# Linear attention, then a mixture of four experts, on one core: values of one chunk and scores of the next in one step, and other dummy products

## The chip, the cores and the metric

The kernel runs on one core of a Trainium2 chip, as one launch. The metric is the device time in microseconds; a comparison takes the median of several runs. The time before is 1175.42 us, the median of three runs.

## The reference

The attention has 4 batches, 8 heads, 768 positions and 64 values a head, and runs over blocks of 64 positions with a state of 64x64 for each head. Its result, brought to 3072 tokens by 512, is the input x of four experts, whose outputs are weighted by normalised probabilities and added. All is float32.

```
for b in range(nb):
    intra = np.einsum('bhic,bhjc->bhij', qb, kb) * Dmask[None]
    intra = np.einsum('bhij,bhjd->bhid', intra, vb)
    inter = np.einsum('bhid,bhde->bhie', qb * lam_pow[None], kv_state)
    out[:, :, sl] = intra + inter
    kv_state = lam_block * kv_state + np.einsum('bhsd,bhse->bhde', kb * rev_pow, vb)
...
for e in range(E):
    h = np.maximum(x @ w1[e], 0.0)
    out += p[:, e:e + 1] * (h @ w2[e])
```

## The kernel before, in words

**Tiling.** The 3072 tokens are three groups of 1024, and a group is eight chunks of 128 positions (two blocks of the reference, all heads): chunks 0 to 7, 8 to 15 and 16 to 23. A unit is one group with one expert; there are twelve. The two products of the experts use recursive schemes with seven products in place of eight: `first_product` (line 974) computes x times w1 in 7 x 7 products, `second_product` (line 1028) the next one in 7, for the first two groups; the last group's second product is nested too (line 1256).

**Time in slots.** The loop over units has seven macro steps (index i) of eight slots (index x), so a unit has 56 slots. Even slots hold a part of the second product of this unit, odd slots a part of the first product of the next unit. Each part is eight records of 128x256 on TensorE, but slot 7, with four. After the parts of a slot, the loop takes at most a few items of vector work from lists (`lately` holds the attention's, `background` and `own_sums` others), then runs the list `steps`, where `attention(g)` has put each chunk's work by slot number.

**A chunk of groups 1 and 2** has these steps. `load_more` loads q and k, `load` loads v. `turn` transposes q and k by TensorE (line 603) into banks s0 and s1, from where ScalarE copies them to qT and kT (lines 611, 612); for chunks 16 to 23, which come through a DRAM tensor in pieces of 32, VectorE does it (`turn_across`, line 585). `decayed` scales k on GpSimd. `scores` does 64x64 products, four at a time in the quarters of the array: q times k (line 633) and the addition to the state (line 640), both into two banks, whose results VectorE masks into the tile st and adds to the state (`mask`, `middle`, `end`). `values` multiplies q scaled with the state (line 687) and st with v (line 705) into two banks; ScalarE copies the results to xc (line 726) and VectorE adds the rest, by the list `adds`, which is emptied at the start of the next step or in a later slot. After each second chunk `pair_sums` does four subtractions on GpSimd and sends the blocks to the DRAM tensor x_blocks (lines 744 to 746).

Before, chunk i of a group is turned at slot BEGIN[g][0] + BEGIN[g][1] * i. Its scores are 4 slots later (6 in group 2), its values 10 (12) slots later, all in banks s0 and s1. q and k are loaded 10 slots ahead of the turn, v 6 slots ahead. `scale_q` multiplies q by its decay: from the bank into a tile qs in group 1, after the transposes into qs in group 2, in both ahead of the scores.

**Operands of a group.** `x_fill` (line 352) loads a group's x from x_blocks on SP's queue, and GpSimd does four subtractions (`x_inner`). It runs in slot 3 of seven macro steps from FILL[g] on. The first product of group 1 begins in macro step 21, which is slot 169.

**Banks.** PSUM has eight banks here: g1 and g3 for the first product, q01, q02, q11, q12 for the second, s0 and s1 for the attention. In the second product, stages M7, M4 and M2 (macro steps 1, 2 and 4) use q02 and q12; the others use q01 and q11.

**Loads.** SP issues nearly all DMAs, in order. In slot 0 of each macro step `feed` loads an operand of w1 (ws_in, line 887) for a later step, ahead of what `steps` has for that slot. `small` takes tiles from a pool of 41 that all parts share.

**The start.** `warm` issues products of zeros on TensorE while the first loads are under way (line 448), ten at first, then three and two between the turns of chunks 0 and 1 and the first scores. Chunks 0 to 7 run ahead of and between the first large products, from a list written out by hand (lines 1436 to 1445).

Of the kernel before, what the change touches and what calls it, by code (L numbers as in the profile page):

```python
# [21 lines left out]
def kernel(  # L22
# [30 lines left out]
    nc = tc.nc  # L53
# [4 lines left out]
    P = nc.NUM_PARTITIONS  # L58
# [4 lines left out]
    CPG = 8  # L63
# [28 lines left out]
    def small(name):  # L92
        return pool.tile([P, W], FP32, name=name, tag="t")
# [44 lines left out]
    nat = {}  # L138
# [272 lines left out]
    def comes_across(n):  # L411
        return where(n)[0] >= SECOND
# [11 lines left out]
    def load_more(n):  # L424
        if not comes_across(n):
            load(n, "qk")
        else:
            trickle(sum(b <= where(n)[1] for b, _ in pieces))
            load_across(n)
            load(n, "k")  # L430
# [8 lines left out]
    load(3)  # L439


    zeros = small("zeros")[:, 0:P]
    nc.vector.memset(zeros, 0.0)

    def warm(n):
        p = bank("g1", "zp")
        for _ in range(n):
            nc.tensor.matmul(out=p[:, 0:P], lhsT=zeros, rhs=zeros, start=True, stop=True)

    warm(10)  # L450

# [32 lines left out]
    def scale_q(qs, of):  # L486
        by = q_decay.unsqueeze(2).to_broadcast([P, NHP, 2, BL])
        tt(nc.vector, by_block(qs), by_block(of), by, ALU.mult)
# [33 lines left out]
    turned, masked = {}, {}  # L522
# [4 lines left out]
    background = []  # L527
# [9 lines left out]
    def take(queue, force=False):  # L537
        for x, f in enumerate(queue):
            if force or getattr(f, "at", 0) <= now[0] and getattr(f, "can", lambda: True)():
                queue.pop(x)()  # L540
                return
# [8 lines left out]
    def soon(n, *work):  # L550

        if n < CPG:
            background[0:0] = work
            rest(len(work))
        else:
            lately.extend(work)

    def decayed(n):

        kn = nat[n, "k"]  # L560
        kd = kn if n >= CPG else small("kd")[:].rearrange("p (h d) -> p h d", d=D)
        nat[n, "kd"] = kd
        by = k_decay.rearrange("p r ac -> p ac r").unsqueeze(3).to_broadcast([P, NHP, 2, D])
        tt(nc.gpsimd, *(x.rearrange("p (ac r) d -> p ac r d", r=2) for x in (kd, kn)), by, ALU.mult)
# [10 lines left out]
    def turn_across(n):  # L575

        qT, kT = nat.pop((n, "qx")), nat.pop((n, "kx"))
        qs = small("qs")

        def scaled():  # L580
            scale_q(qs, qT)
            turned[n] = qT, kT, qs

        def across(x):
            nc.vector.transpose(out=x[:], in_=x[:])
            vector(W, False)

        soon(n, *(lambda x=x: across(x) for x in (qT, kT)), scaled)

    def turn(n, tags):  # L590
        all_added()
        begin_state(n)
        if comes_across(n):
            turn_across(n)
            return
        if n < CPG:
            decayed(n)
        qn, kn = nat.pop((n, "q")), nat[n, "k"]
        qp = bank(tags[0], "qp")
        kp = bank(tags[1], "kp")  # L600
        for x, y in ((qp, qn), (kp, kn)):
            for ac in range(NHP):
                nc.tensor.transpose(  # L603
                    out=x[:, ac * C:(ac + 1) * C], in_=y[:, 2 * ac:2 * ac + 2].rearrange("p r d -> p (r d)"),
                    identity=ident[:],
                )
        if n >= CPG:
            decayed(n)
        del nat[n, "k"]
        qT, kT, qs = small("qT"), small("kT"), small("qs")  # L610
        nc.scalar.copy(out=qT[:], in_=qp[:])
        nc.scalar.copy(out=kT[:], in_=kp[:])
        scaled = lambda: scale_q(qs, qp)
        soon(n, scaled)
        turned[n] = qT, kT, qs, scaled

    def scores(n, tags):
        all_added()
        while n not in turned:
            take(lately, True)  # L620
        qT, kT = turned[n][0:2]
        while any(f in lately for f in turned[n][3:]):
            take(lately, True)
        begin_state(n)
        kd, vn = nat.pop((n, "kd")), nat[n, "v"]
        first, last = where(n)[0] == 0, where(n)[0] == NCH - 1

        sp = [bank(tags[r], "sp") for r in range(2)]
        blk = [slice(x * BL, (x + 1) * BL) for x in range(2)]
        for ac in range(NHP):  # L630
            for r in range(2):
                for x in range(2):
                    nc.tensor.matmul(  # L633
                        out=sp[r][half[x], ac * BL:(ac + 1) * BL], lhsT=hc(kT)[half[r], ac, blk[x]],
                        rhs=hc(qT)[half[r], ac, blk[x]], start=(ac == 0), stop=True, skip_group_check=True,
                    )
        for ac in range(NHP):
            for x in range(1 if last else 2):
                for r in range(2):
                    nc.tensor.matmul(  # L640
                        out=sp[x][half[r], 256 + ac * D:256 + (ac + 1) * D], lhsT=kd[half[x], 2 * ac + r],
                        rhs=vn[half[x], 4 * r + ac], start=False, stop=True, skip_group_check=True,
                    )
        st = small("st")
        added = [sp[x][:, 256:512].rearrange("p (h d) -> p h d", d=D) for x in range(2)]

        def mask(r):
            tt(
                nc.vector, st[:, r * 256:(r + 1) * 256], sp[r][:, 0:256], s_decay[:, r].rearrange("p h c -> p (h c)"),
                ALU.mult,  # L650
            )

        def middle():
            s = states[n][:, 1]
            if first:
                nc.scalar.copy(out=s, in_=added[0])
            else:
                tt(nc.vector, s, s, added[0], ALU.add)

        def end():  # L660
            s = states[after_of(n)] = small("kv")[:].rearrange("p (x h d) -> p x h d", x=2, d=D)
            passed(nc.vector, s[:, 0], states[n][:, 1])
            tt(nc.vector, s[:, 0], s[:, 0], added[1], ALU.add)

        work = [lambda: (mask(0), mask(1)), middle] + ([] if last else [end])
        soon(n, *work)
        masked[n] = st, work

    def values(n, tags):
        all_added()  # L670
        vn = nat.pop((n, "v"))
        qs, *scaled = turned.pop(n)[2:]
        st, work = masked.pop(n)
        while any(f in lately for f in (*scaled, *work)):
            take(lately, True)
        while any(f in background for f in (*scaled, *work)):
            rest(force=True)
        state = states.pop(n)
        first = where(n)[0] == 0
# [67 lines left out]
            made.add(("blocks", g, x)),  # L747
        ))

    FILL = {1: 18, 2: 43}  # L750
    BEGIN = {1: (24, 13), 2: (8 * 19, 22)}
    steps = []

    def attention(g):

        def put(slot, f):
            steps.append((slot, f))

        for i in range(CPG):
            n, s = g * CPG + i, BEGIN[g][0] + BEGIN[g][1] * i  # L760
            put(s - 10, lambda n=n: load_more(n))
            put(s - 6, lambda n=n: load(n, "v"))
            put(s, lambda n=n: turn(n, ("s0", "s1")))
            if comes_across(n):
                put(s - 2, lambda n=n: (decayed(n), nat.pop((n, "k"))))
            put(s + (6 if comes_across(n) else 4), lambda n=n: scores(n, ("s0", "s1")))
            put(s + (12 if comes_across(n) else 10), lambda n=n: values(n, ("s0", "s1")))
            if n == 2 * CPG + 3:
                put(s + 17, turn_gates)
        steps.sort(key=lambda s: s[0])  # L770

    def forget():
# [656 lines left out]
    def loads(*of):  # L1429
        return lambda: [raw_w1(0, x) if isinstance(x, str) else load(x) for x in of]  # L1430
# [3 lines left out]

    h1, h2 = parts["M1"], parts["M2"]
    for f in (
        (ts[0], lambda: warm(3)), (ts[1], lambda: warm(2)), (ss[0], loads(4, 5)), (ss[1], loads("A21", 6)),
        (vs[0], loads("A22")), (vs[1], loads(7)), (ts[2],), (m1[0],), (ss[2],), (m1[2],),
        (vs[2],), (ts[3],), (h2[0][0],), (ss[3],), (ts[4],), (h2[0][1],),
        (vs[3],), (h2[2][0],), (ss[4],), (ts[5],), (h2[2][1], sum_first("S3", "A11", "A21")),  # L1440
        (vs[4],), (h1[1][0],), (ss[5],), (ts[6], sum_first("S1", "A21", "A22", ALU.add)), (h1[1][1],),
        (vs[5],), (h1[3][0],), (ss[6],), (ts[7], load_probs), (h1[3][1], sum_first("S2", "S1", "A11")),
        (vs[6],), (h2[1][0], sum_x(0)), (ss[7],), (h2[1][1], sum_first("S4", "A12", "S2")),
        (begin_chores, m2[3]), (vs[7],), (sum_x(1), quarter_5(0)), (quarter_5(2),),
    ):
        for work in f:
            work()
        now[0] += 1
        pump()
# [178 lines left out]
```

## Time and profile before

| what | us |
|---|---|
| median of three runs (lowest, highest) | 1175.42 (1170.89, 1178.54) |
| the profiled execution, its own time | 1171.55 |
| its span in the profile | 1169.8 |
| TensorE (PE) busy | 1157.8 |
| VectorE (DVE) busy | 791.7 |
| GpSimd (POOL) busy | 646.1 |
| ScalarE (ACT) busy | 271.1 |
| products of zeros, line 448, 30 records | 5.4 |
| transposes of q and k, line 603, 128 records | 19.7 |
| scores, lines 633 and 640, 1472 records | 32.7 |
| values, lines 687 and 705, 1472 records | 32.2 |

The span is that of one execution on the core; its own time is 1.75 us longer. A product in float32 shows as two records, a transpose as one. [...]eight of 128x256 have a mean of 0.38 us each, but start 0.21 us apart. The rate is therefore read from the chain of waits, which gives the time from one step to the next, and not from the mean of a record.

A line of the page's fifth part reads: line, engine, operation, written and read tiles, shapes, count, busy time, mean ns, idle time ahead of it and what ended it. A line of waits reads: engine, line, what it waited for, us in total, times, longest.

### The profile page before, as it was taken

To read this page: it belongs to the slowest core of one execution; us is meant where nothing else is said; L and a number is where in the kernel's file an instruction comes from. 1 tells how busy PE (TensorE), PEld (TensorE's weight loads), DVE (VectorE), ACT (ScalarE), POOL (GpSimd) and SP (SyncE) were. 2 spreads that over 40 slices of the span, in tenths; PEclk is the share of its full clock that TensorE was granted. 3 is DMA by queue.
4 is the path that set the end of the run, shared out by engine and by line. 5 is a ranking of instruction groups with operands and counts; after the bars stand their busy time and mean duration, and the time that the engine had idled before them with its cause. 6 is when DMAs were issued, how large, how long until landed. Compare 5 with 4: busy or idle time off the path is not lost.

```text
span 1169.8 us, 21185 instructions
## 1 busy us (share of the span) xinstructions
PE 1157.8 (99%) x8095; PEld 1006.5 (86%) x8095; DVE 791.7 (68%) x1407; ACT 271.1 (23%) x540; POOL 646.1 (55%) x640
## 2 busy tenths in 40 slices
PE   8999999999999999999999999999999999999998
PEld 7888888888888888888888888888888888888887
DVE  4666895578478567657747836745775666777785
ACT  4321122112211201211211120221233342341231
POOL 2846327546655761065245215655893683882884
PEclk9999999999999999999999999999999999999999
DMA  9884668998997996787868757785765445354442
GB/s 208 219 257 153 185 195 264 289 315 255 310 334 228 311 277 188 221 264 230 247 195 261 243 182 239 215 278 184 252 212 194 140 152 181 129 182 148 154 180 73
DMA packets 265717, 255.63 MB, mean 219 GB/s; under 512 B 121328, under 2 KB 219408, under 8 KB 265616
## 3 DMA queue, kind: packets, MB, share of 16 engines
q1 hardware_dynamic: 254976, 251.46, 69.0%
q10 hardware_dynamic: 10640, 2.82, 1.1%
q8 instruction: 64, 1.05, 0.4%
q14 instruction: 37, 0.30, 0.1%
HBM read 180.80 MB, written 77.61 MB: 221 GB/s over the span
## 4 chain that ended last, share of the span: by engine, by line
PE 95%; DVE 3%; POOL 1%; issue 0%; DMA 0%; ACTq 0%; ACT 0%; POOLq 0%; DVEq 0%
PE pg L974 39%; PE q L1028 31%; PE pq L1256 13%; PE pM L1358 2%; PE pc L1358 2%; DVE m L102 1%; PE sp L633 1%; PE op L687 1%; PE op L705 1%; PE sp L640 1%; PE qp L603 1%; PE kp L603 1%; POOL acc L102 1%; POOL m L102 1%; DVE sums L102 0%
## 5 line engine op out<-in xcount | busy, mean ns | idle before, releaser
L974 PE MATMUL pg<-xs,ws_in 128*128 128x256 f32 x1960 | 471.6, 380 | 0.8 <-DVE m L102 0.7
L1028 PE MATMUL q<-w2t,m 128*128 128x256 f32 x1792 | 424.4, 380 | 0.0
L974 PEld LDWEIGHTS pg<-xs,ws_in 128*128 128x128 f32 x1960 | 369.8, 190 | 53.7 <-DVE m L102 3.3
L102 DVE TENSOR_TENSOR m<-pg,m 128x512 f32<-128x512 f32 x451 | 307.2, 687 | 120.0 <-PE pg L974 109.8
L1028 PEld LDWEIGHTS q<-w2t,m 128*128 128x128 f32 x1792 | 339.3, 190 | 46.6 <-DVE m L102 0.4
L1046 DVE SCALAR_TENSOR_TENSOR acc<-q,gate,acc 128x256 f32<-128x256 f32 x192 | 92.3, 481 | 126.2 <-PE q L1028 125.7
L102 DVE TENSOR_TENSOR m<-m,m 128x512 f32<-128x512 f32 x184 | 152.5, 829 | 7.7 <-ACT m L986 7.7
L986 ACT ACTIVATE m<-m 128x512 f32<-128x512 f32 x132 | 83.0, 630 | 303.6 <-DVE m L102 302.5
L102 POOL TENSOR_TENSOR m<-m,decay 128x512 f32<-128x512 f32 x64 | 81.8, 1293 | 58.1 <-ACT m L986 44.7
L102 DVE TENSOR_TENSOR sums<-pq,sums 128x256 f32<-128x256 f32 x153 | 64.1, 421 | 45.7 <-PE pq L1256 36.9
L982 ACT COPY m<-pg 128x512 f32<-128x512 f32 x88 | 51.5, 585 | 186.1 <-PE pg L974 176.1
L1256 PE MATMUL pq<-acc,w2t 128*128 128x256 f32 x352 | 86.6, 379 | 0.0
L102 POOL TENSOR_TENSOR xs<-xs 128x256 f32<-128x256 f32 x56 | 44.5, 794 | 73.1 <-DMA xs<-x_blocks 57.4
L1256 PEld LDWEIGHTS pq<-acc,w2t 128*128 128x128 f32 x352 | 66.8, 190 | 9.3 <-issue 0.3
L102 POOL TENSOR_TENSOR to<-xc 128x256 f32<-128x256 f32 x16 | 12.5, 783 | 95.8 <-DVE xc L102 67.8
L102 POOL TENSOR_TENSOR acc<-hT,hT 128x512 f32<-128x512 f32 x32 | 40.2, 1269 | 29.7 <-PE pq L1256 27.8
L102 POOL TENSOR_TENSOR kn<-kn,decay 128x512 f32<-128x512 f32 x16 | 18.0, 1123 | 64.6 <-PE kp L603 43.7
L102 POOL TENSOR_TENSOR w2o<-w2b 128x512 f32<-128x512 f32 x32 | 42.4, 1348 | 18.3 <-DMA w2b<-in_moe_w_dram 10.2
L915 ACT ACTIVATE m<-m 128x512 f32<-128x512 f32 x44 | 27.7, 630 | 106.8 <-DVE m L102 106.8
L102 POOL TENSOR_TENSOR ops<-w2b 128x256 f32<-128x256 f32 x24 | 17.8, 764 | 50.7 <-issue 28.2
L102 POOL TENSOR_TENSOR acc<-hT,acc 128x512 f32<-128x512 f32 x32 | 40.7, 1271 | 7.4 <-PE pq L1256 5.4
L102 POOL TENSOR_TENSOR w2o<-w2b,w2o 128x512 f32<-128x512 f32 x24 | 34.2, 1449 | 5.8 <-issue 4.3
(135 smaller groups left out, 1204.8 us busy)
## 6 DMA issues: line engine op xcount, KB each, us to landing
ws_in<-w_ops SPq DMA_DIRECT2D x70, 896.0 KB, 6.3
w2t<-w_ops SPq DMA_DIRECT2D x66, 256.0 KB, 5.1
w2t<-w_sums SPq DMA_DIRECT2D x64, 256.0 KB, 3.7
w_ops<-ops SPq DMA_DIRECT2D x28, 512.0 KB, 4.3
w2t<-in_moe_w_dram SPq DMA_DIRECT2D x48, 256.0 KB, 3.6
w2b<-in_moe_w_dram SPq DMA_DIRECT2D x32, 256.0 KB, 5.5
w_sums<-w2o SPq DMA_DIRECT2D x16, 512.0 KB, 5.7
w2b<-in_moe_w_dram SPq DMA_DIRECT2D x16, 512.0 KB, 7.6
```

Source lines behind the costliest of these rows:

```text
L102: eng.tensor_tensor(out=o, in0=a, in1=b, op=op)
L603: nc.tensor.transpose(out=x[:, ac * C:(ac + 1) * C], in_=y[:, 2 * ac:2 * ac + 2].rearrange("p r d -> p (r d)"), identity=ident[:],)
L633: nc.tensor.matmul(out=sp[r][half[x], ac * BL:(ac + 1) * BL], lhsT=hc(kT)[half[r], ac, blk[x]], rhs=hc(qT)[half[r], ac, blk[x]], start=(ac ...
L640: nc.tensor.matmul(out=sp[x][half[r], 256 + ac * D:256 + (ac + 1) * D], lhsT=kd[half[x], 2 * ac + r], rhs=vn[half[x], 4 * r + ac], start=F ...
L915: nc.scalar.activation(out=o[:], in_=o[:], func=AF.Relu)
L974: nc.tensor.matmul(out=p[:, j * 256:(j + 1) * 256], lhsT=ws[i][:, j * P:(j + 1) * P], rhs=xs[i], start=(fresh and j == 0), stop=True, skip ...
L982: nc.scalar.copy(out=new[at][:], in_=p[:])
L986: nc.scalar.activation(out=new[at][:], in_=new[at][:], func=AF.Relu)
L1028: nc.tensor.matmul(out=p[:, s * DH:(s + 1) * DH], lhsT=h[A_OF[m]][:, c * 256 + s * P:c * 256 + (s + 1) * P], rhs=fed2[g, e, m][uu][:, c], ...
L1046: nc.vector.scalar_tensor_tensor(out=o, in0=x, scalar=w, in1=o, op0=ALU.mult, op1=ALU.add)
L1256: nc.tensor.matmul(out=p[:, 0:256], lhsT=fed3[e, m, x // 2][:, x % 2, c * P:(c + 1) * P], rhs=b[B_OF[i]][:, c * 256:(c + 1) * 256], start= ...
L1358: nc.tensor.matmul(out=p[:, s * 256:(s + 1) * 256], lhsT=a[c][:, f:f + P], rhs=b[:, c, j * 256:(j + 1) * 256], start=(s == 0 and c == 0 an ...
```

## The change

Three edits go together.

- The slots of scores of chunks 8 to 23 are written out in SCORES. For eleven chunks, `both` does the values of the chunk before and then the scores of this one, in one step; those scores use banks q02 and q12. Chunks 8 to 11 and 16 (ALONE) have their scores alone in s0 and s1, and values of a chunk ahead of those, or of a group's last, come 7 slots after its own scores. The turn comes 4 slots ahead of the scores (7 in group 2), q and k are loaded 7 slots ahead of the turn and v 2 slots ahead; in group 2 k is decayed 3 slots ahead of the turn. FILL[1] goes from 18 to 19.
- For chunks 8 to 23, q is scaled in place, from and to SBUF, as the last item of the scores' vector work. The mask writes over kT (over qT in chunks 0 to 7) instead of a tile of its own.
- The products of zeros are 512 columns wide instead of 128. There are three at first instead of ten, then one instead of three, and none instead of two.

```diff
-    zeros = small("zeros")[:, 0:P]
+    zeros = small("zeros")[:]
...
-            nc.tensor.matmul(out=p[:, 0:P], lhsT=zeros, rhs=zeros, start=True, stop=True)
-
-    warm(10)
+            nc.tensor.matmul(out=p[:], lhsT=zeros[:, 0:P], rhs=zeros, start=True, stop=True)
+
+    warm(3)
...
     def turn_across(n):
...
-        qs = small("qs")
-
-        def scaled():
-            scale_q(qs, qT)
-            turned[n] = qT, kT, qs
+        def ready():
+            turned[n] = qT, kT, qT
...
-        soon(n, *(lambda x=x: across(x) for x in (qT, kT)), scaled)
+        soon(n, *(lambda x=x: across(x) for x in (qT, kT)), ready)
...
     def turn(n, tags):
...
-        qT, kT, qs = small("qT"), small("kT"), small("qs")
+        qT, kT = small("qT"), small("kT")
+        qs = small("qs") if n < CPG else qT
...
-        scaled = lambda: scale_q(qs, qp)
-        soon(n, scaled)
-        turned[n] = qT, kT, qs, scaled
+        turned[n] = qT, kT, qs
+        if n < CPG:
+            soon(n, lambda: scale_q(qs, qp))
...
     def scores(n, tags):
...
-        st = small("st")
+        st = kT if n >= CPG else qT
...
         work = [lambda: (mask(0), mask(1)), middle] + ([] if last else [end])
+        if n >= CPG:
+            work.append(lambda: scale_q(qT, qT))
         soon(n, *work)
...
-    FILL = {1: 18, 2: 43}
-    BEGIN = {1: (24, 13), 2: (8 * 19, 22)}
+    FILL = {1: 19, 2: 43}
+    SCORES = {1: (28, 41, 54, 67, 82, 98, 114, 137), 2: (160, 194, 210, 226, 250, 266, 282, 306)}
+    ALONE = *range(CPG, CPG + 4), 2 * CPG
...
-        for i in range(CPG):
-            n, s = g * CPG + i, BEGIN[g][0] + BEGIN[g][1] * i
-            put(s - 10, lambda n=n: load_more(n))
-            put(s - 6, lambda n=n: load(n, "v"))
-            put(s, lambda n=n: turn(n, ("s0", "s1")))
+        def both(n, *tags):
+
+            values(n - 1, ("s0", "s1"))
+            scores(n, tags)
+
+        for i, s in enumerate(SCORES[g]):
+            n = g * CPG + i
+            early = 7 if comes_across(n) else 4
+            put(s - early - 7, lambda n=n: load_more(n))
+            put(s - early - 2, lambda n=n: load(n, "v"))
+            put(s - early, lambda n=n: turn(n, ("s0", "s1")))
             if comes_across(n):
-                put(s - 2, lambda n=n: (decayed(n), nat.pop((n, "k"))))
-            put(s + (6 if comes_across(n) else 4), lambda n=n: scores(n, ("s0", "s1")))
-            put(s + (12 if comes_across(n) else 10), lambda n=n: values(n, ("s0", "s1")))
+                put(s - early - 3, lambda n=n: (decayed(n), nat.pop((n, "k"))))
+            if n in ALONE:
+                put(s, lambda n=n: scores(n, ("s0", "s1")))
+            else:
+                put(s, lambda n=n: both(n, "q02", "q12"))
+            if n + 1 in ALONE or i == CPG - 1:
+                put(s + 7, lambda n=n: values(n, ("s0", "s1")))
             if n == 2 * CPG + 3:
-                put(s + 17, turn_gates)
+                put(s + 10, turn_gates)
...
-        (ts[0], lambda: warm(3)), (ts[1], lambda: warm(2)), (ss[0], loads(4, 5)), (ss[1], loads("A21", 6)),
+        (ts[0], lambda: warm(1)), (ts[1],), (ss[0], loads(4, 5)), (ss[1], loads("A21", 6)),
```

## The prediction

> **What bounds the kernel now.** I read the page first, then the chain of waits, then TensorE's own waits, then single stretches. From the page, busy time by engine, TensorE's slices and granted clock, and the shares of the chain by engine:
>
> ```profile
> PE 1157.8 (99%) x8095; PEld 1006.5 (86%) x8095; DVE 791.7 (68%) x1407; ACT 271.1 (23%) x540; POOL 646.1 (55%) x640
> ...
> PE   8999999999999999999999999999999999999998
> ...
> PEclk9999999999999999999999999999999999999999
> ...
> PE 95%; DVE 3%; POOL 1%; issue 0%; DMA 0%; ACTq 0%; ACT 0%; POOLq 0%; DVEq 0%
> ```
>
> TensorE is the limit in every slice, at full clock. Its waits (engine, line, releaser, us, times, longest) are small; these are the two longest:
>
> ```profile
> PE op L705 <- issue: 3.1, 2, 2.3
> PE zp L448 <- DVE zeros L443: 1.1, 1, 1.1
> ```
>
> So only less TensorE time, or a new stall of TensorE, can move the end. What the attention costs there is seen in the chain between 150 and 240 us (start, us, what):
>
> ```profile
> 158.50 1.73 PE pg L974 x8
> 160.22 0.62 PE sp L633 x32
> 160.85 0.47 PE sp L640 x32
> 161.31 1.93 PE q L1028 x8
> 163.24 1.73 PE pg L974 x8
> ...
> 171.31 0.62 PE op L687 x32
> 171.94 0.47 PE op L705 x32
> 172.40 1.92 PE q L1028 x8
> ```
>
> Eight large products take 1.73 us, but 1.93 just after a step of small 64x64 ones. Of such a step's two equal halves, the first takes 0.62 and the second 0.47. Entering small products costs 0.15 us and leaving them 0.20. The chain in the first 20 us has two scores steps with nothing between:
>
> ```profile
> 9.72 0.62 PE sp L633 x32
> 10.35 0.47 PE sp L640 x32
> 10.81 0.47 PE sp L633 x32
> 11.28 0.54 PE sp L640 x32
> ```
>
> The second step's first half is 0.47: joined steps pay the entry once.
>
> [...]0.15 + 0.20 us per visit, and none between steps of one size. [...]the dummy products from 1.05 us on start 213 ns apart until 3.98 us and 111 ns apart after. [...]The trace has 64 such transfers of 16 KB, and TensorE's three waits inside small products, at 12.5, 19.8 and 44.4 us, come after 448, 704 and 1984 of its records, that is 448 + 256n, and end 1.4 us after the end of a transfer.
>
> **The change, part by part.**
>
> *Merged steps.* Chunks 8 to 23 run inside the large products. Of their 16 scores, those of 8, 9, 10, 11 and 16 stay alone; 11 follow the values of the chunk before directly. Before there are 32 visits to small products, after 16 + 5 = 21 (the five values before a lone scores, or last, stay alone). Each removed visit saves 0.15 + 0.20 = 0.35 us: 11 x 0.35 = 3.9 us. The products and transposes are the same in number. A joined step is 256 instructions in 2.2 us, but after 130 us each block of instructions, by that count, came over 6 us ahead of its use. I take the 3.9 whole, since every visit lies on TensorE's path; its bounds are 0 (different banks or the order of half tiles spoil the join) and 11 x 0.38 = 4.2 us (from the starts of the large products around a step, 1.30 us a step, against 0.92 us of steady small products).
>
> *Scores in banks q02 and q12.* The second product uses them in stages M7, M4 (macro steps 1 and 2) and M2 (4). Merged scores stand at slots 26, 42, 2 and 25 of the 56 of a unit, where the next fresh use is 6, 22, 6 and 7 slots away. VectorE must have read the scores by then: mask, middle, end, one item a slot, three slots. Eight slots last 7 x 1.73 + 0.86 = 13.0 us, so a slot is 1.62 us and the spare is three slots, 4.9 us. I cost it at nothing; with VectorE three slots behind, TensorE would wait in each such step.
>
> *The sums after values* are now put on VectorE's queue at once (scores first empties that list), not a slot later. They wait for ScalarE's copies (0.27 us each, four in 0.8 us). Behind them stand only evictions of products that TensorE issues after the scores, 1.1 us later. Nothing; bounds 0 and 0.5 us a step.
>
> *Scaling of q.* It moves behind the scores and, for group 1, reads SBUF: 0.82 (the median of qs from qx) instead of 0.69 us (qs from qp), eight times, about 1 us of VectorE, which waits for TensorE 126 us in one group of rows alone. Nothing; if VectorE were the limit, 1 us. In group 2 it leaves the stretch at 366 to 379 us where the chain does run over VectorE and TensorE loses 0.8 us in gaps; up to 0.8 us gained, of which I take half, 0.4. In-place scaling and masking save buffers only.
>
> *Loads.* q and k go out 7 slots before the turn instead of 10. v goes out 2 before the turn instead of 6: 6 slots before the scores instead of 10 in group 1, 9 instead of 12 in group 2. Landing times (min, median, max) of k and of v in 120 to 660 us:
>
> ```profile
> DMA to landing us min/median/max: 2.5/4.9/7.5
> ```
>
> ```profile
> DMA to landing us min/median/max: 3.0/5.9/8.2
> ```
>
> Seven slots are 11.3 us, but SP's queue is in order and sometimes waits for the weights. SP between 186 and 196 us (start, us, engine, line, operation):
>
> ```profile
> 189.38 0.38 SPq L213 DMA_DIRECT2D w_ops<-ops  x1
> ...
> 194.36 0.32 SPq L887 DMA_DIRECT2D ws_in<-w_ops  x1
> 194.73 0.43 SPq L147 DMA_DIRECT2D vn<-in_v_dram  x1
> ```
>
> The ws_in load of slot 56 waits 4.1 us for w_ops to land. Chunk 11's q and k, now at slot 56, stand right behind it. Their last of four issues comes at about 196.5, landing at 201.4 (median) or 204.0 (slowest); the turn, still at slot 63, needs k at 202.4. Chunk 10's v, now at slot 48, stands behind the ws_in load that went out at 178.9: it lands at 185.2 or 187.5, needed at 186.2. So two places with 1.0 us to spare at the median, and 1.6 and 1.3 us too late at the slowest. I take +1.0 us in all; bounds 0 and 8 us (half a us at each of 16 chunks). In group 2, GpSimd's decay of k follows its load after 4 slots, 6.5 us, instead of 8. It may hold GpSimd's queue some 2 us a time, but k is first needed 10 slots later, and GpSimd is busy 55%.
>
> *Operands of group 1.* Its values now end at slot 144 instead of 125, and its filling starts one macro step later (slot 155). The fill that stood at slot 155 before was issued at 368.8 and its four GpSimd subtractions were done at 384.5; slot 169, where the first is now needed, begins at about 393.7: 9.2 us of cover. From the values of chunk 15 on TensorE to the last write of its block were 319.9 to 329.3 us, plus about 5 to land (as the other loads): 14.4 us. From the end of slot 144 (351.2 us) that gives 365.6, ahead of the fill at 368. Nothing.
>
> *Dummy products.* Ten of 128 columns become three of 512, 2560 columns become 1536, but each is issued as two passes: 20 x 128 against 6 x 512. At half clock a pass of 512 takes four times 213 ns, at full clock four times 111. With the rise after 2.93 us as before: 3.4 passes slow, 2.6 fast, about 4.1 us against 3.93. They end near 5.4 us, after a longer memset; the first turn waits for q until 5.69 anyway, and the k after it until 6.90. Later, three become one (0.67 to 0.89 us, +0.2) and two vanish (-0.45). Sum -0.2; bounds -0.5 and +1.
>
> **Sum.** -3.9 - 0.4 + 1.0 - 0.2 = -3.5 us. On the profiled execution: 1171.55 - 3.5 = 1168.0, its span 1169.8 - 3.5 = 1166.3. The median of runs is 1175.42, 3.9 above that execution; the same step gives 1171.9. That is 0.3%, less than the 1% that a measurement of this kernel can surely tell from no change (three runs span 7.7 us).
>
> **Rivals.**
> *Loads come late* (0.20): the queue's waits above recur and TensorE stands at turns or scores. For it: the two places with about 1 us to spare. Against it: elsewhere SP kept within three slots of its plan. Price 3 to 8 us in place of 1.0: 1174 to 1179.
> *The join saves nothing* (0.04): [...]Against it, the two scores in a row at 9.72. Then -3.5 + 3.9: 1175.8.
> *Slower* (0.12): GpSimd or SP hands over group 1's operands late at slots 169 to 217, because values 19 slots later are followed by a fill only 8 slots later. The wait of SP for x_blocks would hold weights too. It has some 2.5 us until the fill and 9.2 us behind it; each us beyond 11.7 costs one. It decides (over 1%, 11.8 us) from 11.7 + 11.8 + 3.5 = 27 us of lateness on; the time then is 1188 or more. Against it: GpSimd is idle 45%, and a forced write goes ahead of the other chores.
> *Faster by over 1%* (0.03): would need 8 us beyond the sum, more than TensorE's waits in these units hold; only a drift of the runs gives it, 1163.
>
> **How the numbers follow.** The likeliest case (0.61) gives 1171.9, its own range 1168 to 1176 by the runs' spread. With late loads and no saving the range is 1166 to 1180. Faster by over 1%: 0.03; slower by over 1%: 0.12; within 1%: 0.61 + 0.20 + 0.04 = 0.85.
>
> **What would show it.** Right: chains of 0.62, 0.47, 0.47, 0.47 with values and scores together 11 times, one 1.93 after each; TensorE busy about 4 us less; no wait of sp or op for q banks. Wrong: TensorE waiting on DMA for qn, kn or vn (late loads), pg waiting for GpSimd's xs near slot 169 (slower rival), a first scores half of 0.62 behind values (no saving), or gaps before q of M2 or M7.

## The result, and the profile after

The kernel after takes 1182.49 us (median of 7 runs, 1180.49 to 1183.9) against 1174.47 us for the kernel before in 7 runs beside it: 1.0064 times as long, 95% interval 1.0037 to 1.0092. The forecast was 1171.9, with a range of 1166 to 1180: the time moved the other way and lies above it. The profiled execution takes 1182.4 us, its span is 1180.6, 10.8 more than before. In the code after, the lines are: scores 629 and 636, values 685 and 703, turns 600, the first product's 983, the second's 1037, the load of v 147.

The page of the kernel after, busy time by engine and the chain's shares by engine:

```profile
PE 1160.5 (98%) x8073; PEld 1006.2 (85%) x8073; DVE 793.5 (67%) x1407; ACT 270.7 (23%) x540; POOL 649.6 (55%) x640
...
PE 90%; DVE 6%; DMA 1%; POOL 1%; issue 1%; SPq 1%; ACT 0%; DVEq 0%; POOLq 0%
```

TensorE had 95% of the chain before and has 90% now; VectorE went from 3% to 6%, and DMA and SP's queue appear with 1% each. TensorE's waits between 130 and 500 us, the kernel after:

```profile
PE pg L983 <- DVE m L102: 2.6, 4, 1.5
PE sp L636 <- DMA vn<-in_v_dram: 2.3, 1, 2.3
PE q L1037 <- DVE m L102: 1.2, 1, 1.2
PE qp L600 <- PE q L1037: 0.8, 1, 0.8
PE qp L600 <- DMA across<-in_q_dram: 0.3, 1, 0.3
```

The same stretch of the kernel before:

```profile
PE pg L974 <- DVE m L102: 0.7, 3, 0.3
PE qp L603 <- issue: 0.2, 1, 0.2
```

So 0.9 us of waits became 7.2, of three kinds: for v to land, for VectorE's m, and at two turns of q and k.

To place the loss I took from each trace the starts of the large products, and so the time of every slot, numbered from the first. The times of stretches of slots (us; slots 0 to 4, 8.0 before and 7.6 after, are left out; "rest" is from slot 440 to the end of the span):

| kernel | start | 4-56 | 56-112 | 112-168 | 168-208 | 208-224 | 224-280 | 280-336 | 336-440 | rest | 4-440 |
|---|---|---|---|---|---|---|---|---|---|---|---|
| before | 86.40 | 93.12 | 105.40 | 99.02 | 68.60 | 27.19 | 98.48 | 95.78 | 168.45 | 319.29 | 756.04 |
| after | 91.11 | 96.11 | 103.43 | 99.29 | 66.97 | 33.37 | 98.13 | 96.36 | 168.85 | 319.33 | 762.50 |

The units that the attention runs in (slots 4 to 440) take 6.46 us more, and what follows them takes the same. The start takes 4.7 more here, but it is between 86.4 and 93.5 us over all fourteen profiles, with the old dummies and the new; the last section says why. The stretch from 4 to 440 is the better measure, and I use it below. It is one execution for each kernel. The kernel before with other dummies alone (e2 below) takes 755.42 there, 0.6 less than before: slots 4 to 56 are the same to 0.01 us, and single slots after 87 differ by up to 0.4. So a difference of under 1 us in the whole stretch says little, while one in a slot of the first hundred can be trusted where two pairs of runs show it.

**The largest single loss.** The chain of the kernel after around 470 us (start, us, what):

```profile
441.77 0.62 PE op L685 x32
442.39 0.47 PE op L703 x32
442.86 0.47 PE sp L629 x32
443.33 0.47 PE sp L636 x32
443.79 1.93 PE pg L983 x8
...
469.89 0.67 PE op L685 x32
470.56 0.02 SPq L147
470.58 0.03 issue
470.61 2.99 DMA vn<-in_v_dram
473.60 0.14 issue
473.74 0.68 PE sp L636 x16
474.42 3.28 PE pg L983 x8
```

The first five lines are a joined step as forecast: 0.62, 0.47, 0.47, 0.47, then one 1.93. The joined step of values of chunk 17 and scores of chunk 18 breaks in the middle. Its scores need v of chunk 18, which SP issued only at 470.61, after the values of the same step had read their first operands (`op L685`). The load was planned for slot 201, and SP stood before it for 15.2 us. SP's issues in between:

```profile
455.02 0.36 SPq L1057 DMA_DIRECT2D out_dram<-acc  x1
470.61 0.38 SPq L147 DMA_DIRECT2D vn<-in_v_dram  x1
471.05 0.58 SPq L402 DMA_DIRECT2D across<-in_q_dram  x1
```

SP's own waits name the cause (us in total, times, longest):

```profile
SPq L147 <- PE op L685: 22.3, 2, 15.2
```

The load of v waits for TensorE to end `op L685`, the product of chunk 17's scaled q and its state: the tile that v takes over from the shared pool is one that the values of chunk 17 read. Before, those values came six slots after their own scores. Joined, they wait for the scores of chunk 18, and these wait for v: the load is held until the very step that needs it. The last line of the chain shows a second price: eight large products take 3.28 us instead of 1.93. From 474.84 to 478.25 us the granted clock is half, the only time in the units, and the products start 427 ns apart instead of 216 (8 x 0.21 = 1.7 us). Slot by slot, against e3 below, the wait for v takes 2.5 us, the half clock 1.7, and at slot 216 (484 to 487 us) large products wait 1.0 us for VectorE, which the late scores had made late.

### The profile page after: what moved, and what is told of

Read it like the earlier page. It is cut to its first block, busy times and chain, and to the rows that moved or that the text cites. A ratio compares the mean times of both kernels' runs of the same rounds, so it can differ in the third digit from the quotient of the medians.

```text
span 1180.6 us, 21149 instructions
## 1 busy us (share of the span) xinstructions
PE 1160.5 (98%) x8073; PEld 1006.2 (85%) x8073; DVE 793.5 (67%) x1407; ACT 270.7 (23%) x540; POOL 649.6 (55%) x640
## 4 chain that ended last, share of the span: by engine, by line
PE 90%; DVE 6%; DMA 1%; POOL 1%; issue 1%; SPq 1%; ACT 0%; DVEq 0%; POOLq 0%
PE pg L983 37%; PE q L1037 29%; PE pq L1265 13%; DVE m L102 3%; PE pM L1367 3%; PE pc L1367 2%; PE op L685 1%; PE sp L629 1%; PE sp L636 1%; PE op L703 1%; PE qp L600 1%; PE kp L600 1%; PE zp L448 1%; POOL acc L102 1%; POOL m L102 0%
## 5 line engine op out<-in xcount | busy, mean ns | idle before, releaser
L1265 PE MATMUL pq<-hT,w2t 128*128 128x256 f32 x144 | 37.0, 379 | 0.0
```

Of the source, the lines that this page charges most:

```text
L1265: nc.tensor.matmul(out=p[:, 0:256], lhsT=fed3[e, m, x // 2][:, x % 2, c * P:(c + 1) * P], rhs=b[B_OF[i]][:, c * 256:(c + 1) * 256], start= ...
```

## The experiments

Each table row gives the slots 4 to 440 of the profiled execution; a ratio is against runs of the kernel before on the same chip, with its 95% interval.

| run | 4-440, us | median, us (runs) | before beside it, us | ratio |
|---|---|---|---|---|
| e1_old_dummies | 760.97 | 1182.43 (8) | 1175.72 | 1.0071 [1.0043, 1.0099] |
| e2_dummies_alone | 755.42 | 1175.74 (14) | 1175.72 | 1.0008 [0.9991, 1.0025] |
| e3_values17_apart | 757.70 | 1178.21 (22) | 1175.72 | 1.0017 [1.0003, 1.003] |
| e4_quarter_scale | 762.88 | 1182.49 (9) | 1175.72 | 1.0065 [1.0041, 1.0089] |
| e5_no_scale | 754.94 | 1173.08 (12) | 1176.96 | 0.9994 [0.9973, 1.0014] |
| e6_scale_on_gpsimd | 758.35 | 1178.19 (20) | 1176.96 | 1.0017 [1.0004, 1.003] |
| e7_scale_later | 756.24 | 1176.52 (20) | 1176.96 | 0.9999 [0.9986, 1.0013] |
| e8_scale_from_bank | 755.63 | 1177.11 (12) | 1176.96 | 1.0005 [0.9987, 1.0024] |
| e9_bank_and_values_early | 753.48 | 1173.87 (22) | 1174.89 | 0.9991 [0.998, 1.0002] |
| e10_no_merging | 759.53 | 1178.29 (8) | 1174.89 | 1.0038 [1.0022, 1.0053] |
| e11_mixed_scale | 759.72 | 1180.28 (7) | 1174.89 | 1.005 [1.0033, 1.0067] |
| e12_mixed_scale_values_at_7 | 756.77 | 1175.53 (22) | 1174.89 | 1.0012 [1.0001, 1.0024] |

I had three causes in mind, and expected each to cost a part: the dummies, by a longer time at half clock in the start (about 4 us), v of chunk 18 (about 4), and VectorE's moved scaling. The rival to all of them was that the joined steps themselves crowd VectorE.

**The dummy products.** The kernel after with the old ones:

```
-    warm(3)
+    warm(10)
...
-        (ts[0], lambda: warm(1)), (ts[1],), (ss[0], loads(4, 5)), (ss[1], loads("A21", 6)),
+        (ts[0], lambda: warm(3)), (ts[1], lambda: warm(2)), (ss[0], loads(4, 5)), (ss[1], loads("A21", 6)),
```

(with the 128 columns of before), and the kernel before with only the new ones, the reverse edit.

> The changed kernel with the dummy products of before (ten of 128 columns, then three and two). Theory: the wide dummies keep TensorE at half clock for the whole start, so this run's clock rises near 4 us and not 7 us, the first slot of the units begins near 87 us instead of 91, and the time is about 4 us below the changed kernel's 1182.5: 1178.5. Rival: the late rise is luck of a clock window that runs by itself, whatever the dummies are; then 1182 +- 2 and rises that vary from run to run.

> The kernel before with the dummy products of the change and nothing else. Theory: about +4 us over before, 1178.5, with the loss complete before 91 us and no new waits after. Rival (luck of the window): 1174.5 +- 2. As predicted at first: -0.2 us.

Both came as their rival had it, and the dummies fall as a cause: 1182.43 with the old ones beside 1182.49, and 1.0008 for the new ones alone, with an interval that includes no change. In e1 the clock did rise at 4.07 us instead of 7.21, and still the first slot began at 92.8 us, later than the 91.1 of the kernel after.

e1 shows one thing more, since from slot 4 on it is the kernel after. v is late in it in the same way:

```profile
476.53 0.68 PE L636 MATMUL sp<-vn,kn 64*64 64x64 f32 x16 [2.35 <-DMA vn<-in_v_dram]
```

The clock stays full here, and slots 208 to 224 take 31.69 us instead of 33.37. So 1.7 us is what the half clock costs, and it does not always follow the wait; the last section says why.

**Values of chunk 17 apart from the scores of chunk 18**, all else as after:

```
-    ALONE = *range(CPG, CPG + 4), 2 * CPG
+    ALONE = *range(CPG, CPG + 4), 2 * CPG, 2 * CPG + 2
```

> The changed kernel with the values of chunk 17 apart from the scores of chunk 18, 7 slots after their own scores. Theory: the 41 tiles of the pool are all in use when v of chunk 18 is to be loaded, so SP holds it until the values of chunk 17 free one; with those values earlier the load goes out on time, the wait of 2.3 us on it and the window of half clock behind it (1.65 us) vanish, one saving of 0.36 us is lost: 1182.5 - 3.6 = 1179. Rival: the load is late because the queue of SP is late in general; then the wait stays, within 1 us of the changed kernel.

Slots 208 to 224 take 27.18 us instead of 33.37, as before the change (27.19). The chain of this run at the same place:

```profile
453.50 0.62 PE op L685 x32
454.12 0.47 PE op L703 x32
454.59 1.93 PE q L1037 x8
...
469.46 0.62 PE sp L629 x32
470.09 0.45 PE sp L636 x16
470.54 1.93 PE pg L983 x8
```

and SP's issue of v in it:

```profile
454.22 0.38 SPq L147 DMA_DIRECT2D vn<-in_v_dram  x1
```

The median is 1178.21, near the expected 1179. v still waits for the same reader: it goes out 0.1 us after `op L685` ends at 454.12. But that reader now stands 15 us ahead of the scores at 469.46, the load is hidden, and the half clock is gone too. The stretch 4 to 440 loses 4.80 us although one join (0.36) is given up, so this wait with its consequences cost 5.2 us. The ratio falls from 1.0064 to 1.0017. Which tile v takes over is read from SP's wait and from this run. Whether the pool of 41 had no other free tile, as the expectation has it, or this tile was only the next in turn, is not shown; a larger pool was not tried.

**How the scaling of q costs time.** The kernel of e3 still takes 757.70, 1.7 more than before, though ten joins stand. In the chain of the kernel after TensorE waits for VectorE here:

```profile
175.46 1.71 DVE qT L102
177.17 1.04 DVE m L102
178.21 0.04 issue
178.25 1.13 PE q L1037 x4
```

and the timeline shows what ran beside it:

```profile
173.63 2.99 POOL L102 TENSOR_TENSOR w1o<-w1b 128x512 f32<-128x512 f32 x2 [6.01 <-PE pg L983]
175.38 1.79 DVE L102 TENSOR_TENSOR qT<-qT,decay 128x512 f32<-128x512 f32 x1
```

Scaling in place takes 1.79 us, most of it while GpSimd works, and the m that the second product waits for stands behind it. Its durations (min/median/max ns) in place in chunks 8 to 15, and from the bank in chunks 0 to 7:

```profile
L102 DVE TENSOR_TENSOR qT<-qT,decay x8: 677/828/1793, 149.5 to 353.7; 128x512 f32<-128x512 f32 x8
```

```profile
L102 DVE TENSOR_TENSOR qs<-qp,decay x8: 682/688/692, 8.2 to 49.8; 128x512 f32<-128x512 f32 x8
```

Of the eight in place, the two with no operation of GpSimd beside them take 677 and 682 ns, the other six 811 to 1793. Of the eight from the bank, the three with GpSimd at work all the while take 682 to 685. Two large groups of this trace divide in the same way: `m<-m,m`, with both inputs in SBUF, takes 673 to 693 ns in the 86 cases without GpSimd beside it and 674 to 1787 (median 903) in the 82 with GpSimd at work for over half of the time; `m<-pg,m`, with one input from a bank, takes 650 to 693 ns in 170 cases without and 648 to 694 in 249 with. If it were VectorE's own time that counts, a quarter of the columns should free most of it (the rest of q of chunks 8 to 23 is left unscaled; otherwise the kernel after):

```
-            work.append(lambda: scale_q(qT, qT))
+            def part():
+                o = by_block(qT)[:, 0:1]
+                by = q_decay[:, 0:1].unsqueeze(2).to_broadcast([P, 1, 2, BL])
+                nc.vector.tensor_tensor(out=o, in0=o, in1=by, op=ALU.mult)
+                vector(W, False)
+            work.append(part)
```

> The changed kernel, but for chunks 8 to 23 the scaling of q covers a quarter of its columns (the rest is left unscaled, so part of the computation is left out). Theory: the scale item, five slots behind the scores, puts VectorE behind where large products wait for it; with a quarter of it the waits of TensorE for VectorE in the units (5.6 us in the changed kernel's profile) fall to 1 us or less: 1177 to 1178. Rival: VectorE is late by all five items of a joined step together, or by loads; then at most 1 us is gained.

```profile
174.25 2.99 POOL L102 TENSOR_TENSOR w1o<-w1b 128x512 f32<-128x512 f32 x2 [6.01 <-PE pg L989]
...
176.00 1.40 DVE L666 TENSOR_TENSOR qT<-qT,decay 128x128 f32<-128x128 f32 x1
```

This missed: the whole is no faster (762.88, and 1182.49 where 1177 to 1178 was expected). The trace shows why. A quarter of the work, which takes 0.28 us at the least among the eight, took 1.40 us here and ended at 177.40, just after GpSimd's pair ended at 177.24. Of its record, 1.24 us lie beside that pair and 0.16 behind it, over half of the 0.28. I read this as VectorE standing still until the pair ended, and not as an even sharing; that is an inference from this one record. Then four runs on top of e3, in one comparison. No scaling at all of chunks 8 to 23 (it is left out; `vector(W, False)` only keeps the program's own count of VectorE's work, by which it places other items):

```
-            work.append(lambda: scale_q(qT, qT))
+            work.append(lambda: vector(W, False))
```

> Values of chunk 17 apart (as in e3_values17_apart), and no scaling of q at all for chunks 8 to 23 (part of the computation is left out; the place in the order of vector work is kept). Theory: what is left of the loss is the scaling itself. From and to SBUF it waits for GpSimd's operation to end (in e4 128 columns took 1.40 us and ended 0.16 us behind GpSimd's), so a shorter one did not help and none at all does: the waits of TensorE for VectorE in the units fall from 5.3 us (e3's profile) to at most 1.5 us, and the time to about 1174. Rival: the other four items at the new slots are too much for VectorE by themselves; then at least 3 of the 5.3 us stay.

Scaling on GpSimd:

```
-            work.append(lambda: scale_q(qT, qT))
+            def scaled():
+                by = q_decay.unsqueeze(2).to_broadcast([P, NHP, 2, BL])
+                tt(nc.gpsimd, by_block(qT), by_block(qT), by, ALU.mult)
+            work.append(scaled)
```

> Values of chunk 17 apart, and the scaling of q of chunks 8 to 23 done by GpSimd in place of VectorE. If VectorE's own time or its waiting in the scaling is the cause, TensorE's waits for VectorE fall to about 2 us, 1175. Rival: GpSimd's scaling then holds up VectorE's other operations that read SBUF twice, and nothing is gained: 1178.

Scaling in place, but not earlier than six slots after the scores:

```
-            work.append(lambda: scale_q(qT, qT))
+            work.append(after(6, lambda: scale_q(qT, qT)))
```

> Values of chunk 17 apart, and the scaling of q at least 6 slots behind the scores instead of about 4 (right behind the other items). If it only stands at a bad place, just ahead of operands that large products wait for, the waits at slots 46 to 48 of a unit fall by half or more: 1176. Rival: it meets GpSimd's operations elsewhere as well: 1178 +- 1.

Scaling of chunks 8 to 15 from the bank into a tile of its own, ahead of the scores, as before the change:

```
-        qs = small("qs") if n < CPG else qT
+        qs = small("qs")
...
-        turned[n] = qT, kT, qs
-        if n < CPG:
-            soon(n, lambda: scale_q(qs, qp))
+        scaled = lambda: scale_q(qs, qp)
+        turned[n] = qT, kT, qs, scaled
+        soon(n, scaled)
...
+        while any(f in lately for f in turned[n][3:]):
+            take(lately, True)
...
-        if n >= CPG:
+        if n >= 2 * CPG:
```

> Values of chunk 17 apart, and for chunks 8 to 15 q scaled as before the change: from the PSUM bank, into a tile of its own, ahead of the scores. Theory: reading PSUM it does not wait for GpSimd (0.69 us each, before), so the waits in group 1 at 150, 176 and 284 us (3.65 us) vanish, those of group 2 (0.9 us at 577) stay: about 1174.5. Rivals: the extra tile for each chunk fills the pool and makes a new wait elsewhere in group 1; or the place of the item was not the cause and 1178 stays.

The medians of e5 and e7 came near what was expected (1174 and 1176), and e6 as its rival had it (1178). Against e3's 757.70, leaving the scaling out saves 2.76 us, taking it from the bank 2.07, doing it later 1.46; on GpSimd it costs 0.65 more, since k's decay there then comes late and TensorE waits 1.4 us for it in `sp L636`. Not all of this is the scaling of group 1. Of e8's 2.07 us, 1.4 lie in slots 34 to 105, where that scaling has its effect, and 0.7 in slots 272 and 384, which e8's edit doesn't touch. Of the 2.76 without any scaling, 2.4 lie in those slots of group 1. So the new place and source cost 1.4 to 2.4 us there, though VectorE is idle a third of the time. The whole-run intervals of e5, e7 and e8 include 1 and overlap with e3's; the split between them rests on the profiles.

e8 gained less than the 3.65 us that I expected, and its trace shows the reason. With the scaling gone from there, another operation with both inputs in SBUF meets the same pair of GpSimd and takes 1.47 instead of 0.68 us; TensorE then waits 0.8 us for m:

```profile
171.11 2.94 POOL L102 TENSOR_TENSOR w1o<-w1b 128x512 f32<-128x512 f32 x2 [5.95 <-DVE kv L102]
...
171.45 1.47 DVE L102 TENSOR_TENSOR m<-m,m 128x512 f32<-128x512 f32 x1
```

**Lone values six slots after their scores**, the kernel of e8 otherwise:

```
-                put(s + 7, lambda n=n: values(n, ("s0", "s1")))
+                put(s + 6, lambda n=n: values(n, ("s0", "s1")))
```

> The kernel with the values of chunk 17 apart, with the scaling of chunks 8 to 15 taken from the PSUM bank ahead of the scores as before the change, and besides with every lone values step 6 slots after its scores instead of 7, so that the next turn stands three slots behind it and not two. If the turns at 183.7 and 208.9 us wait (0.94 and 0.42 us) because VectorE has not yet emptied the bank that the lone values filled, these waits go and slots 4 to 440 take about 754.4 us, 1.2 less than the 755.6 of the run without this edit; the median is then about 1176 beside 1177 of the kernel before. If the turns wait for q and k to land or for ScalarE, the waits stay and the stretch stays at 755.6.

753.48, 2.15 less than e8, where 1.2 was expected. The two waits at turns (0.7 and 0.3 us in e8) are gone; TensorE's waits between 95 and 600 us in this run:

```profile
PE pg L985 <- DVE m L102: 1.1, 2, 0.6
PE pg L985 <- DVE xs L102: 0.6, 1, 0.6
PE sp L638 <- issue: 0.2, 1, 0.2
```

In the change the next turn stands two slots behind lone values and takes their bank. In the kernel after VectorE empties it just ahead of the turn, behind two operations on m:

```profile
183.01 1.28 DVE L102 TENSOR_TENSOR m<-pg,m 128x512 f32<-128x512 f32 x2
184.21 0.47 DVE L102 TENSOR_TENSOR xc<-xc,op 128x128 f32<-128x128 f32 x2
...
184.90 0.63 PE L600 MATMUL qp<-ident,qn 128*128 128x128 f32 x4 [0.78 <-PE q L1037]
```

The wait is put down to TensorE itself, which had long been done; the end of `xc` is what precedes the turn. Slot by slot, the three turns at slots 37, 50 and 63 gain 0.2, 0.9 and 0.5 us. Another 0.8 us comes at slot 46, for a reason I had not looked for: with lone values at slot 48, GpSimd takes the pair w1o ahead of the four subtractions that follow the values, and so it meets VectorE's work as above. At slot 47 the subtractions come first, as before the change, and the pair goes later (181.29 us in the kernel before). In e9:

```profile
186.15 2.49 POOL L102 TENSOR_TENSOR w1o<-w1b 128x512 f32<-128x512 f32 x2
```

So the meeting of scaling and GpSimd at 175 us in the kernel after rests on both edits, and whether scaling in place would cost as much there with values at six slots was not run. The kernel of this run takes 0.9991 [0.998, 1.0002] of before: the shortest time of the kernels that do all the work, but the interval includes no change.

**No joins**, the kernel of e8 otherwise:

```
-    ALONE = *range(CPG, CPG + 4), 2 * CPG, 2 * CPG + 2
+    ALONE = range(CPG, 3 * CPG)
```

> As the run with the scaling of chunks 8 to 15 from the bank, but no chunk's scores join the values of the chunk before: every scores step of groups 1 and 2 stands alone and its values come 7 slots later. If the join saves 0.36 us at each of the 10 places that this run takes apart, slots 4 to 440 take 3.6 us more, 759.2 instead of 755.6 us, and the median is about 1181. If the join saves nothing and the early turns, late loads and queues of VectorE are all that counts, the stretch stays within 1 us of 755.6.

759.53, 3.90 more than e8 for ten joins. Slot by slot each of the ten is 0.36; the other 0.3 lies in single slots that no join touches. The ratio rises from 1.0005 to 1.0038. The join itself works, and its price is as forecast; the rival that joined steps crowd VectorE falls.

**All mended with few tiles**: as e9, but chunks 12 to 23 scaled in place six slots later (`n < 16` becomes `n < 12`, and `after(6, ...)` for the rest), and the same with lone values at 7 slots.

> All causes found, mended together with few tiles: values of chunk 17 apart, lone values 6 slots after their scores, scaling of chunks 8 to 11 from the bank ahead of the scores, and of chunks 12 to 23 in place but at least 6 slots after them. If the parts add up, slots 4 to 440 take 753.5 to 754.5 us, 2 us less than the kernel before, and the median is about 0.15% below it. If the scaling late in group 1 falls on other work of VectorE and GpSimd, the stretch takes 755 to 756.5 us, as in the run with the scaling later alone.

> As the run with all causes mended, but with the lone values at 7 slots after their scores as the change has them. If the turns two slots behind them wait for VectorE, slots 4 to 440 take 1.0 to 1.4 us more than in that run, with TensorE's waits at the turns near 183.7 and 208.9 us back; if not, within 0.3 us of it.

Here my theory missed. e12 takes 756.77 and e11 not less but 2.95 more. Values six slots behind the scores meet the scaling that is held back for six: it becomes due in the very step that needs it. e11 near 354 us:

```profile
355.15 0.68 DVE L102 TENSOR_TENSOR qT<-qT,decay 128x512 f32<-128x512 f32 x1
```

```profile
355.98 0.75 PE L687 MATMUL op<-qT,kv 64*64 64x64 f32 x32 [1.60 <-ACT m L997]
```

The product that reads qT starts 0.15 us after the scaling ends, having waited 1.60 us (the profile names ACT, which isn't what was missing). TensorE waits so three times, at 354, 454 and 651 us, 1.5 to 1.6 us each. So the whole stretch of e12 against that of e11 doesn't measure the turns. Slots 4 to 56 alone do, ahead of these waits: 93.12 us with six slots (e11) and 95.02 with seven (e12), as 93.36 (e9) and 95.02 (e8), with the same gains at slots 37, 46 and 50.

## Why the prediction was wrong, point by point

The parts of 762.50 - 756.04 = +6.46 us, each from a pair of runs, forecast beside them:

| part | forecast | measured | from |
|---|---|---|---|
| eleven joins | -3.9 | -4.0 | 0.36 a join: the large products move by 2.22 us for a joined step and by 1.29 for a lone one; ten are 3.90 in e10 less e8 |
| v of chunk 18 late, with half clock | +1.0 for all loads | +5.2 | after less e3, plus the join given up |
| scaling of q behind the scores | -0.4 | +2.1, of which 1.4 in group 1's slots | e3 less e8 |
| lone values at 7, turns behind them | 0 | +2.15, of which 1.5 at turns, 0.8 at slot 46 | e8 less e9 |
| not resolved | | +1.0 | e9 less before, plus ten joins |

The parts add up by construction, since each run starts from the last. The two rows on scaling and on lone values aren't independent: GpSimd's pair stands behind some of each.

**Merged steps: right**, in kind and size: ten of the eleven joined steps run as forecast, and 0.36 us each is the 0.35 of the sum. No wait for `issue` stands at one in the kernel after: between 95 and 600 us TensorE has none, 0.2 us before. One sign did not come: TensorE is busy 2.7 us more, not 4 less; but e2, with other dummies alone, is busy 2.5 more than before too, so that sign could not show the join.

**Banks q02 and q12: right**: no wait of scores or of the second product for these banks appears.

**Loads: the step that failed.** I asked when SP's queue would come to each load and when it would land, and took +1.0 with the two places at chunks 10 and 11. No load is late there: the turn of chunk 11 waits 0.3 us, but for its bank, since the wait is gone in e9. I did not ask whether the tile that v takes over would be free when v's turn came. The sentence "In-place scaling and masking save buffers only" stopped at the savings: the joined step lengthens the life of a chunk's state and operands until the next chunk's scores. What the runs showed in place of a late queue is a load held 15.2 us for a tile, at one chunk, and 5.2 us of loss. The bound of 8 us held this outcome, but the chance for it was put on the queue, and neither the half clock behind the wait (1.7 us) nor VectorE's lateness after it (1.0) was in the price.

**Scaling of q: failed too.** "Nothing; if VectorE were the limit, 1 us" used VectorE's idle time over a whole group. What counted was its place: the fourth item behind the scores, ahead of the m that TensorE needs next, and from SBUF, where it took up to 1.1 us longer beside GpSimd (1.79 instead of 0.68). Of the 0.4 us to be gained in group 2, the kernel after shows 0.3: at slots 156 to 165 TensorE loses 0.7 us beside the small products, 1.0 before. But it then waits on VectorE at 576 us (slot 272), 0.7 in e9 and 0.4 even in e5, which leaves the scaling out.

**Sums after values: failed.** "Behind them stand only evictions": true, but ahead of them stand others, and I looked only at what the sums delay and not at who waits for the bank that they free, the turn two slots on. That lone values move from six slots behind their scores to seven has no line of its own in the sum. The turns are 1.5 of the 2.15 us; the 0.8 at slot 46 is GpSimd's pair, which the moved values let in ahead.

**Dummies: right** as far as it can be told; -0.2 is below what the start varies. The working has two flaws that carry nothing: ten products of 128 are 1280 columns and not 2560, and the clock's rise, taken to stay 2.93 us behind the first product (about 4.4 us), came at 4.3 to 7.2 us in the twelve profiles with the new dummies.

**Rivals.** "Loads come late" happened in kind, at one chunk, by a cause I hadn't named, and more happened beside it. The slower rival by group 1's operands did not: no large product waits for an operand at slots 169 to 217, and slots 168 to 208 take 66.97 us after 68.60, by the 1.6 us of small products that now stand elsewhere.

**What stays open.** 1.0 us of the units. It is the difference of waits in single slots: e9 loses 1.6 us at slots 102 to 105 and 0.8 at slot 272, most of it in waiting for VectorE, where the kernel before loses nothing, and the kernel before 1.0 at slots 156 to 165 and 0.4 at 89 to 99, where e9 loses nothing. What sets these is not traced. Open is also whether the start is longer by the change. The whole runs are 0.64% slower, some 7.5 us of 1174, where the units explain 6.5; one profile each can't settle the start.

## What to carry to other kernels

Joining two steps saves the switch at their border (here 0.36 us), but it also moves the last read of everything the first step uses to the second one's time: follow the tiles, and ask whether the second step's own load waits for a tile that only the first step frees. Idle share of an engine prices nothing for a moved operation: look at what stands right behind it in its queue, who waits for that, and what GpSimd runs beside it at that moment (a scaling of 0.68 us took up to 1.79 here). When a bank's reader is a queue of vector work, keep a slot more between its producer and the next user.

## What the runs showed of the hardware

**A wait of 2.29 us was followed by half clock.** The granted clock changes on a grid of 3.413 us in all fourteen traces: in the kernel after at 7.21, 17.45, 20.87, 474.84 and 478.25 us, 3, 1, 133 and 1 of such windows apart. In each window of that grid I summed TensorE's idle time by the profile, gaps of over 0.1 us alone. Up to the last product the clock fell from full to half 18 times in the fourteen, and the window ahead was never idle for more than 2.60 us. In the kernel after these windows were idle for 1.90 and 2.29 us; in the kernel before the fullest was idle for 1.67 us, and the clock stayed full. Of the windows at full clock, all 13 with 1.86 us or more were followed by half clock, five of the seven between 1.63 and 1.86, and none with less. So in these traces the fall came with TensorE idle for about half a window; the ends of its records are modelled, so the border is good to some tenths. Half clock lasted one window in 16 cases and two in the others (e1 and e7); where large products run, a window cost some 1.7 us (products 427 ns apart instead of 216; slots 208 to 224 in 33.37 us beside 31.69 in e1).

What followed a wait of 2.3 us differed with its place on the grid. In the kernel after, 2.29 us of the wait for v lay within one window, and half clock followed. In e1 the same wait of 2.35 us lay across a border at 475.11, 0.9 us before it and 1.4 behind it, and nothing followed. So it was in the kernel before, with a wait of 2.3 us at 12.7 us and 1.7 in the fuller window.

**Why the start varies.** TensorE waits in its small products up to 2.3 us at a time in the kernel before, 2.1 in the kernel after and 2.6 in e9. In the traces of before, after, e1 and e3 these waits end 1.3 to 1.6 us after the end of a 16-KB transfer of instructions, from which I take it that they are waits for instructions; the profile puts them down to `issue`, so this is my estimate. The start was the longer the more windows of half clock it held: 86.4, 88.3 and 89.4 us with none, 88.6 to 91.6 with one, 92.0 to 92.8 with two, 93.5 with three. The number doesn't follow the dummies: none and two in the two profiles with the old ones (before and e1), none to three with the new. No run changed these waits alone, so this is read from the traces and not tested.

**The record of the short scaling ended just behind GpSimd's.** VectorE's record of the 128-column scaling lasted 1.40 us, twice that of 512 columns undisturbed (0.68) and five times its own least (0.28): it ended 0.16 us behind GpSimd's pair, so I take it that the record includes a wait for GpSimd. The profile names no releaser for it.
